# Attention, routed experts and a dense layer on one core: the second head pair's operands packed like the later pairs', and its q and k transposed ahead of the first scores

## The chip, the cores and the metric

The kernel runs on one core of a Trainium2 chip. The metric is the device time of one execution in microseconds, the median of several runs. TensorE is called PE here, VectorE DVE, ScalarE ACT, GpSimd POOL, SyncE SP.

## What is computed

Three layers follow one another: causal attention with a bias, a mixture of eight experts of which each token takes one, and a dense layer with a squared ReLU. The change touches only the attention, of which this is the core (B = 4 batches, H = 8 heads, S = 576 tokens, D = 64):

```python
scores = scale * np.matmul(q, k.transpose(0, 1, 3, 2))
cum = np.cumsum(np.maximum(s, 0.0), axis=-1)
bias = -(cum[:, :, :, None] - cum[:, :, None, :])
scores = np.where(causal, -1000000000.0, scores + np.minimum(bias, 0.0))
attn = np.exp(scores - np.max(scores, axis=-1, keepdims=True))
attn = attn / (np.sum(attn, axis=-1, keepdims=True) + 1e-09)
return np.matmul(attn, v).astype(np.float32)
```

## The kernel before

**Tiling.** Two heads of a batch make a pair; there are 16 pairs, numbered 0 to 15 in the code (pair 0 is called the first here, pair 1 the second). A pair's 576 query rows are cut into blocks of 128, and the blocks of both heads into seven units, run in the order `order=[0, 1, 3, 11, 2, 10, 4]`: units 0 and 1 hold the block of both heads, units 2, 3, 10 and 11 one block of one head, and unit 4 holds the last rows of both heads, the tail, in a PSUM tile of two banks (`ps_2`, tag `s2`, one buffer). A unit runs through scores on PE (`emit_s`), mask and maximum on DVE (`emit_m`), exponential on ACT (`emit_e`), transposes on PE (`emit_t`), their copy to SBUF (`emit_v`); then come the products with v (`emit_pv`), and the output of the pair is transposed and stored.

**Operands.** q and k are loaded by `load_qk` (six DMA issues a pair), transposed on PE in three parts (`qk_pe`: q, k, and the tails of both), and split by `qk_hi` on ACT and `qk_lo` on DVE into a rounded part and its remainder, so that fp32r matmuls give scores with enough digits. `st_a` (three buffers) and `st_b` (two) hold them. For pairs below `ND = 2` the 64 rows of a head and the rows of the other lie side by side: q of head 0 stands in the upper half of `st_a`, q of head 1 in the lower half of `st_b`, the other halves are set to zero on POOL, and a score block takes four passes: high by high, high by low, low by high, and one with `cum_q` and `cum_k` that adds the bias. From pair 2 on each head has high and low parts stacked over all 128 partitions with the rows of the bias from DRAM beside them (`aug_d`), so that two passes do. To get there, `copy_b` copies head 1's rows to `st_b` on POOL, `spread_b` and `spread_a` move 64 partitions to the other 64 by DMA (288 KB each), and `load_aug` fetches the bias rows of a head. `spread_a` overwrites rows that `spread_b` and `copy_b` read.

**Order.** The order on every engine is written out by hand: `at(key, fn)` notes a step, and `emit_tasks` emits all steps by rising key; each engine runs its own in that order, and SP issues its DMAs in that order, waiting in place for what a DMA needs. A pair has seven keys; pair p's first score has the key 7p - 2.85. The preparation (constants, running sums, the first pair's operands, loads of the second pair's q and k and of v) stands ahead of all keys; warm-up matmuls on ones fill PE's pauses there. With the keys of before, SP runs behind the preparation: q and k of pair 2 (-9.83) and pair 3 (-3.99), the gate weights `wp` (0.3, in `init_rest`), q and k of pair 4 (3.01), v of pair 2 (3.59), `load_aug` for head 1 and `spread_b` of pair 2 (6.11 and 6.16), q and k of pair 5 (7.01), `spread_a` and `load_aug` for head 0 of pair 2 (9.66). Pair 1's q and k are transposed between the first pair's units (0.87, 2.16 and 2.43), from PSUM tiles of the ring of three with the tag `t`.

Of the kernel before, what the change touches and what calls it, by code (L numbers as in the profile page):

```python
# [12 lines left out]
F32 = mybir.dt.float32  # L13
# [11 lines left out]
P = 128  # L25
# [57 lines left out]
    xt0=2.2,  # L83
    xt1=1.3,
    hv=0.9,
    q1=4.32,
)


# [1 line left out]
def attention_moe_ffn_kernel(  # L91
# [22 lines left out]
    SP = NB * P  # L114
    HP = H // 2
    NPAIR = B * HP
    ND = 2
    NO = K_['NO']
    MC = NT // P
    CAPS = [352, 320, 304, 304, 288, 288, 272, 256]  # L120
# [52 lines left out]
    def new_half(pool, key, slot):  # L173
        halves[key] = pool.tile([P, 2, 4096], F32R, tag=slot, name=slot)
# [42 lines left out]
    def at(key, fn, *args):  # L217
        tasks.append((key, len(tasks), fn, args))
# [232 lines left out]
    with tc.manual_schedule():  # L451
        with ExitStack() as actx:
# [37 lines left out]
            def bank(r):  # L490
                if r == "s":
                    return ps_s.tile([P, 512], F32, tag="s", name="s")
                if r == "o":
                    return ps_o.tile([P, 512], F32, tag=o_tag, name=o_tag)
                return ps_t.tile([P, 512], F32, tag="t", name="t")
# [46 lines left out]
            qk_ps = {}  # L542

            def qk_pe(pp, part):
                ps = qk_ps[pp, part] = bank(K_["ring"][part])
                if part < 2:
                    t = raw_q[pp][:, part * QM:(part + 1) * QM]
                    for c in range(NB - 1):
                        nc.tensor.transpose(ps[:, c * P:(c + 1) * P], t[:, c * P:(c + 1) * P], ident)  # L549
                else:  # L550
                    nc.tensor.transpose(ps[:, 0:2 * TAIL], raw_q.pop(pp)[:, 2 * QM:], ident)
# [556 lines left out]
            with tc.tile_pool(name="prep", bufs=1) as prep:  # L1108
# [50 lines left out]
                for a in range(2):  # L1159
                    nc.gpsimd.memset(rs_t[a], 1.0)  # L1160
                for a in range(2):
                    nc.gpsimd.memset(st_b[a][0:64, 1].bitcast(F32), 0.0)
                nc.gpsimd.memset(carry, 0.0)
                nc.gpsimd.memset(carryb, 0.0)
                nc.gpsimd.memset(tbl, 0.0)
                nc.gpsimd.memset(wp, 0.0)
                nc.gpsimd.memset(st_a[1][64:128, 0:3:2].bitcast(F32), 0.0)
                nc.gpsimd.memset(st_b[1][0:64, 0:3:2].bitcast(F32), 0.0)
                load_qk(1)
                load_v(0)  # L1170
                for part in range(3):
# [5 lines left out]
                        qk_lo(0, part)  # L1177
                qk_lo(0, 2)
                for r in range(2 * ND):
                    if r < ND:  # L1180
                        nc.scalar.activation(
                            out=cum_q[:, r], in_=cum_r.bitcast(F32), func=AF.Copy, scale=sel[:, r:r + 1])
                    else:
                        nc.gpsimd.tensor_scalar(
                            out=cum_q[:, r], in0=cum_r.bitcast(F32), scalar1=sel[:, r:r + 1], scalar2=None,
                            op0=ALU.mult)
                nc.scalar.copy(out=tri, in_=mt)
                nc.scalar.copy(out=iota_r, in_=ii)
                nc.scalar.copy(out=iota8, in_=ii[:, 0:E])
                nc.scalar.copy(out=iota8p, in_=ii[:, E:2 * E])  # L1190
                nc.sync.dma_start(out=aug_d[0].rearrange("c r t -> (c r) t"), in_=cum_k.bitcast(F32))
                nc.sync.dma_start(
                    out=aug_d[1, 0:2].rearrange("c r t -> (c r) t"), in_=cum_r[0:2 * NH].bitcast(F32))
# [12 lines left out]
            def init_rest():  # L1206
# [9 lines left out]
                nc.vector.tensor_single_scalar(out=ij, in_=ij, scalar=63, op=ALU.bitwise_and)  # L1216
                nc.vector.tensor_copy(out=idab[:, :, :, 1], in_=ij)
                nc.vector.memset(idab[TAIL:P, :, NB - 1], 0.0)
                for hd in range(2):
                    for i, w in enumerate((w_gate, w_ogate)):  # L1220
                        nc.sync.dma_start(
                            out=wp[64 * hd:64 * hd + 64, :, 16 * hd + 8 * i:16 * hd + 8 * i + 8],
                            in_=w.rearrange("(j h p) e -> h p j e", h=2, p=64)[hd])
# [4 lines left out]
                oT.extend(more[:, a] for a in range(NO - 2))  # L1228

            at(0.3, init_rest)  # L1230
            new_half(wpool1, (0, "a"), "w0")
            new_half(wpool1, (0, "b"), "w1")

# [2 lines left out]
            at(NU * ND + 0.5, init_spare)  # L1236

            def early(pp):
                return min(NU, 3 * max(pp - ND, 0))

            for pp in range(NPAIR):
                base = NU * pp
                t0 = base - NU
                if pp >= 2:
                    at(max(t0 + K_["ldqk"] - early(pp), t0 - 2 * NU + K_["scq"] - early(pp - 2) + 0.2), load_qk, pp)
                    at(t0 + K_["ldv"], load_v, pp)
                if pp >= 1:
                    if pp >= ND:
                        at(t0 + K_["sck"] - early(pp), scale_tail, pp, nc.gpsimd)
                    else:  # L1250
                        at(K_["od"][0], scale_tail, pp, nc.vector)
                    for part in range(3):
                        tq = t0 + K_["qk"][part] - early(pp) + (0 if pp >= ND else K_["q1"])
                        at(tq, qk_pe, pp, part)
                        at(tq + K_["qkh"], qk_hi, pp, part)
                        at(tq + K_["qkl"], qk_lo, pp, part)
                if pp >= ND:
                    tb = t0 + max(K_["dup"], K_["qk"][2] + K_["qkl"] - early(pp) + 0.4)
                    at(tb - 0.05, load_aug, pp, 1)
                    at(tb - 0.04, copy_b, pp)  # L1260
                    at(tb, spread_b, pp)
                    at(tb - K_["dup"] + K_["dupa"], spread_a, pp)
                    at(tb - K_["dup"] + K_["dupa"], load_aug, pp, 0)
                end = pp == NPAIR - 1
                units, vact, pv = (K_["l" * end + nm] for nm in ("order", "vact", "pv"))
                for i, un in enumerate(units):
# [557 lines left out]
```

## Time and profile before

| what | value |
|---|---|
| median of three runs | 862.3 us (861.71 to 862.62) |
| the profiled execution's own time | 862.74 us |
| its span | 861.0 us |
| PE busy | 843.1 us, 98% |
| DVE, ACT, POOL busy | 520.4, 452.3, 262.1 us |
| first scores of the pairs 0, 1, 2, 3 begin at | 8.94, 24.05, 39.38, 52.16 us |
| attention's scores end at about | 215 us |

Times in the rows are microseconds from the span's start. In a timeline a row is an instruction, or several of one kind merged, with its start and its duration; matmuls are pipelined, so that the difference of two starts tells more than a duration. SPq stands for SP's queue of DMA issues. The granted clock of a stretch is the share of PE's clock that the chip let through.

### The profile page before, as it was taken

The page shows a single profiled execution, that of the slowest core. Times are in us where ns is not written, and L with a number is a line of the kernel's source. Part 1 is how long each engine was busy: PE and PEld are TensorE (multiplying, and loading weights), DVE is VectorE, ACT ScalarE, POOL GpSimd, SP SyncE. Part 2 cuts the span into 40 slices and gives each one's busy share as a digit, 9 for nine tenths or more (in the row PEclk, how much of TensorE's full clock was granted, in tenths as well). Part 3 has the DMA queues.
Part 4 walks back from the last instruction along what each step waited for, and adds up shares of the span by engine and source line. Part 5 has one row for each costly group of instructions (what it writes and reads, how often), then busy time and mean ns, then how long its engine had stood idle before and what let it go on. Part 6 is the DMA issues. An engine that isn't in the chain of part 4 may idle for free.

```text
span 861.0 us, 15161 instructions
## 1 busy us (share of the span) xinstructions
PE 843.1 (98%) x5412; PEld 748.7 (87%) x5412; DVE 520.4 (60%) x1180; ACT 452.3 (53%) x1012; POOL 262.1 (30%) x304
## 2 busy tenths in 40 slices
PE   8999999999999999999999999999999999999995
PEld 6876777777799999999999999999999999999994
DVE  7667777978777677768976767664233343232221
ACT  7787878988465446566655545443233232233221
POOL 6322334543126465566422232331101011001001
PEclk9999999999999999999999999999999999999999
DMA  7676677753287898999983433321010121001001
GB/s 168 137 162 142 144 183 180 178 127 91 78 278 232 255 252 266 233 280 274 296 246 96 147 120 101 100 84 62 13 62 37 37 75 38 1 1 37 1 0 40
DMA packets 113029, 113.14 MB, mean 131 GB/s; under 512 B 66034, under 2 KB 83954, under 8 KB 112947
## 3 DMA queue, kind: packets, MB, share of 16 engines
q1 hardware_dynamic: 104962, 96.68, 42.1%
q0 software_dynamic: 3664, 9.62, 3.3%
q10 hardware_dynamic: 4320, 5.80, 2.0%
q8 instruction: 45, 0.74, 0.4%
q14 instruction: 38, 0.30, 0.1%
HBM read 80.50 MB, written 23.32 MB: 121 GB/s over the span
## 4 chain that ended last, share of the span: by engine, by line
PE 47%; issue 31%; DVE 6%; ACT 6%; POOL 5%; DMA 4%; POOLq 1%; SPq 0%; ACTq 0%; DVEq 0%
PE z L1431 14%; PE z L1482 7%; PE z L1473 6%; PE s L636 5%; PE t L733 5%; PE t L696 4%; DMA cv<-in_moe_w_out_dram 2%; ACT p L680 2%; POOL out_dram L1541 1%; DVE w L250 1%; POOL cvm L1400 1%; PE t L549 1%; POOL cvm L1399 1%; ACT sta L576 1%; DMA w_out_d<-cvm 1%
## 5 line engine op out<-in xcount | busy, mean ns | idle before, releaser
L1431 PE MATMUL z<-xt,w 128*128 128x384 f32 (+6 forms) x1920 | 329.7, 320 | 0.7 <-DVE h L1442 0.6
L1431 PEld LDWEIGHTS z<-xt,w 128*128 128x128 f32 x1920 | 308.1, 188 | 9.8 <-DVE h L1442 1.2
L1482 PE MATMUL z<-w,h 128*128 128x512 f32 x864 | 214.9, 393 | 0.0
L1482 PEld LDWEIGHTS z<-w,h 128*128 128x128 f32 x864 | 160.7, 188 | 29.3
L1451 DVE SCALAR_TENSOR_TENSOR r<-z,r 128x384 f32<-128x384 f32 x96 | 53.3, 556 | 127.2 <-ACT r L1450 127.2
L1450 ACT ACTIVATE r<-z 128x384 f32<-128x384 f32 x96 | 47.2, 492 | 150.3 <-PE z L1431 149.3
L1473 PE MATMUL z<-h,w 128*128 128x304 f32 (+5 forms) x768 | 111.3, 294 | 0.4 <-DVE h L1442 0.2
L1473 PEld LDWEIGHTS z<-h,w 128*128 128x128 f32 x768 | 104.0, 189 | 1.2 <-ACT h L1441 0.4
L1399 POOL TENSOR_TENSOR cvm<-cvm,cva 128x512 f32<-128x512 f32 x32 | 43.5, 1361 | 170.6 <-DVE cva L1395 121.9
L1541 POOL DMA_INDIRECT out_dram<-ysb,tok_m x18 | 17.4, 969 | 245.5 <-ACT ysb L1528 183.2
L1458 DVE TENSOR_TENSOR h<-r,h 128x384 fp32r<-128x384 f32 x96 | 61.0, 636 | 50.3 <-ACT h L1457 49.7
L680 ACT ACTIVATE p<-p,nm 128x128 f32<-128x128 f32 (+3 forms) x144 | 84.3, 590 | 3.7 <-DVE nm L663 2.3
L1457 ACT CAST h<-r 128x384 fp32r<-128x384 f32 x96 | 49.3, 513 | 64.1 <-DVE r L1451 63.8
L250 DVE TENSOR_TENSOR w<-stg,w 128x1024 fp32r<-128x1024 f32 x49 | 75.1, 1534 | 5.4 <-ACT w L246 5.4
L663 DVE CUSTOM_DVE_ANT_0 p<-s,mask 128x128 f32<-128x128 f32 (+3 forms) x128 | 59.7, 486 | 30.4 <-PE s L636 29.3
L696 PE MATMUL t<-ident,p 128*128 128x128 f32 x400 | 69.1, 283 | 2.8 <-DVE sta L580 1.1
L246 ACT CAST w<-stg 128x1024 fp32r<-128x1024 f32 x49 | 51.4, 1049 | 22.0 <-POOL cvm L1400 18.2
L696 PEld LDWEIGHTS t<-ident,p 128*128 128x128 f32 x400 | 44.4, 140 | 18.7 <-ACT p L680 6.2
L597 POOL CAST stb<-sta 64x1152 fp32r<-64x1152 f32 x28 | 31.4, 1150 | 79.7 <-PE s L636 46.3
L1400 POOL TENSOR_TENSOR cvm<-cvs,cvm 128x512 f32<-128x512 f32 x32 | 54.2, 1694 | 2.5
L636 PE MATMUL s<-sta 128*64 128x288 f32 (+4 forms) x204 | 50.0, 342 | 0.9 <-DVE sta L580 0.9
L715 ACT COPY pt<-t 128x512 f32<-128x512 f32 (+1 forms) x94 | 47.0, 515 | 7.3 <-PE t L733 4.1
(242 smaller groups left out, 1024.8 us busy)
## 6 DMA issues: line engine op xcount, KB each, us to landing
stg<-in_moe_w_dram SPq DMA_DIRECT2D x42, 512.0 KB
cv<-in_moe_w_out_dram SPq DMA_DIRECT2D x16, 512.0 KB
stx<-in_moe_w_dram SPq DMA_DIRECT2D x14, 512.0 KB
cv<-in_moe_w_in_dram SPq DMA_DIRECT2D x14, 512.0 KB
xr<-yT_d SPq DMA_DIRECT2D x8, 768.0 KB
qk<-in_q_dram SPq DMA_DIRECT2D x32, 128.0 KB
v<-in_v_dram SPq DMA_DIRECT2D x32, 128.0 KB
stg<-in_moe_w_dram SPq DMA_DIRECT2D x16, 256.0 KB
```

The lines of the kernel that those rows point to most:

```text
L250: nc.vector.tensor_tensor(out=lo, in0=raw.pop(job), in1=hi.bitcast(F32), op=ALU.subtract)
L636: nc.tensor.matmul(ps[0:mw, d0:d0 + nn], lhsT=ql[r, m0:m0 + mw], rhs=kl[r, c0:c0 + nn], start=(i == 0 and (tail or n == 0)), stop=(done an ...
L663: nc.vector.tensor_tensor_reduce(out=dst, in0=src, in1=msk, scale=-1.0, scalar=3.0e38, op0=ALU.add, op1=ALU.min, accum_out=nm[:, c:c + 1])
L680: nc.scalar.activation(out=pt[:, cs], in_=pt[:, cs], func=AF.Exp, scale=-1.0, bias=nm[:, c:c + 1], accum_out=rs[:, r:r + 1])
L696: nc.tensor.transpose(tp[:, i * P:(i + 1) * P], pt[:, j0:j0 + P], ident)
L1399: nc.gpsimd.tensor_tensor(out=m, in0=m, in1=a.bitcast(F32), op=ALU.mult)
L1400: nc.gpsimd.tensor_tensor(out=m, in0=sq, in1=m, op=ALU.add)
L1431: nc.tensor.matmul(ps[:, 0:n], lhsT=wa[:, zw, kk, fl * P:(fl + 1) * P], rhs=xt[:, zx, kk, 0:n], start=(i == 0), stop=(i == 3 * KD - 1))
L1451: nc.vector.scalar_tensor_tensor(out=gg, in0=ps[:, 0:TT], scalar=0.0, in1=gg, op0=ALU.max, op1=ALU.mult)
L1458: nc.vector.tensor_tensor(out=ht[:, 1], in0=gg, in1=ht[:, 0].bitcast(F32), op=ALU.subtract)
L1473: nc.tensor.matmul(y_acc[g][d][:, 0:n], lhsT=wb[:, zw, fl, d * P:(d + 1) * P], rhs=ht[:, zh, 0:n], start=(f == 0 and i == 0), stop=(f == n ...
L1482: nc.tensor.matmul(acc, lhsT=ht[:, zh, c * P:(c + 1) * P], rhs=wb[:, zw, fl, :], start=(first and i == 0), stop=(last and i == 2))
```

## The change

`ND` becomes 1: only the first pair keeps the four passes, and the second is packed as all later ones. Its zeros are no longer set, `cum_q` holds two rows instead of four, both made on ACT, and four small casts of constants move from ACT to POOL. `st_b`'s second buffer gets a wider stretch of zeros. The second pair's q and k are transposed with the keys -2.87 and -2.86, just ahead of the first score (-2.85), into the two banks of the tail's PSUM tile; their high and low parts and the tails follow up to -0.15. Its moves get keys from -0.9 to -0.08 in the order `load_aug` for head 1, `copy_b`, `spread_b`, `spread_a`, `load_aug` for head 0. The load of pair 3's q and k moves from -3.99 to 0.5, and the gate weights from 0.3 to 2.0. The spare output buffers, which reuse `cum_q`'s memory, are made at 7.5 instead of 14.5. Keys of later pairs stay.

```diff
-    q1=4.32,
+    q1=[[-2.87, -2.84, -2.15], [-2.86, -1.2, -1.1], [-1.0, -0.2, -0.15]],
...
-    ND = 2
+    ND = 1
...
             def qk_pe(pp, part):
-                ps = qk_ps[pp, part] = bank(K_["ring"][part])
+                if pp == 1 and part < 2:
+                    if part == 0:
+                        qk_ps[pp] = ps_2.tile([P, 1024], F32, tag="s2", name="s2")
+                    ps = qk_ps[pp][:, 512 * part:512 * part + 512]
+                else:
+                    ps = bank(K_["ring"][part])
+                qk_ps[pp, part] = ps
...
-                    nc.gpsimd.memset(st_b[a][0:64, 1].bitcast(F32), 0.0)
+                    nc.gpsimd.memset(st_b[a][0:64, 1:2 + a].bitcast(F32), 0.0)
...
-                nc.gpsimd.memset(st_a[1][64:128, 0:3:2].bitcast(F32), 0.0)
-                nc.gpsimd.memset(st_b[1][0:64, 0:3:2].bitcast(F32), 0.0)
...
                 for r in range(2 * ND):
-                    if r < ND:
-                        nc.scalar.activation(
-                            out=cum_q[:, r], in_=cum_r.bitcast(F32), func=AF.Copy, scale=sel[:, r:r + 1])
-                    else:
-                        nc.gpsimd.tensor_scalar(
-                            out=cum_q[:, r], in0=cum_r.bitcast(F32), scalar1=sel[:, r:r + 1], scalar2=None,
-                            op0=ALU.mult)
-                nc.scalar.copy(out=tri, in_=mt)
-                nc.scalar.copy(out=iota_r, in_=ii)
-                nc.scalar.copy(out=iota8, in_=ii[:, 0:E])
-                nc.scalar.copy(out=iota8p, in_=ii[:, E:2 * E])
+                    nc.scalar.activation(
+                        out=cum_q[:, r], in_=cum_r.bitcast(F32), func=AF.Copy, scale=sel[:, r:r + 1])
+                nc.gpsimd.tensor_copy(out=tri, in_=mt)
+                nc.gpsimd.tensor_copy(out=iota_r, in_=ii)
+                nc.gpsimd.tensor_copy(out=iota8, in_=ii[:, 0:E])
+                nc.gpsimd.tensor_copy(out=iota8p, in_=ii[:, E:2 * E])
...
+            def load_wp():
...
+            at(2.0, load_wp)
...
             def early(pp):
-                return min(NU, 3 * max(pp - ND, 0))
+                return min(NU, 3 * max(pp - 2, 0))
...
-                    at(max(t0 + K_["ldqk"] - early(pp), t0 - 2 * NU + K_["scq"] - early(pp - 2) + 0.2), load_qk, pp)
+                    tq = max(t0 + K_["ldqk"] - early(pp), t0 - 2 * NU + K_["scq"] - early(pp - 2) + 0.2)
+                    at(0.5 if pp == 3 else tq, load_qk, pp)
...
-                    if pp >= ND:
+                    if pp >= 2:
                         at(t0 + K_["sck"] - early(pp), scale_tail, pp, nc.gpsimd)
...
                     for part in range(3):
-                        tq = t0 + K_["qk"][part] - early(pp) + (0 if pp >= ND else K_["q1"])
+                        if pp == 1:
+                            for t1, fn in zip(K_["q1"][part], (qk_pe, qk_hi, qk_lo)):
+                                at(t1, fn, pp, part)
+                            continue
+                        tq = t0 + K_["qk"][part] - early(pp)
...
                 if pp >= ND:
                     tb = t0 + max(K_["dup"], K_["qk"][2] + K_["qkl"] - early(pp) + 0.4)
-                    at(tb - 0.05, load_aug, pp, 1)
+                    if pp == 1:
+                        tb = K_["q1"][2][2] + 0.05
+                    at(tb - 0.05 if pp > 1 else -0.9, load_aug, pp, 1)
                     at(tb - 0.04, copy_b, pp)
                     at(tb, spread_b, pp)
-                    at(tb - K_["dup"] + K_["dupa"], spread_a, pp)
-                    at(tb - K_["dup"] + K_["dupa"], load_aug, pp, 0)
+                    ta = tb - K_["dup"] + K_["dupa"]
+                    if pp == 1:
+                        ta = tb + 0.02
+                    at(ta, spread_a, pp)
+                    at(ta, load_aug, pp, 0)
```

## Rows read from the trace of the kernel before

**Rows 1.** The page: each engine's busy us, share, instructions.

```profile
PE 843.1 (98%) x5412; PEld 748.7 (87%) x5412; DVE 520.4 (60%) x1180; ACT 452.3 (53%) x1012; POOL 262.1 (30%) x304
```

**Rows 2.** Stretches by pair: length, engines' busy us (count), granted clock, DMA share, GB/s.

```profile
24.00:39.40 15.40, 15.40 (x124) 13.28 (x122) 9.70 (x33) 10.98 (x32) 5.60 (x7) 1.00 0.71 155
39.40:52.20 12.80, 12.02 (x99) 9.70 (x96) 8.65 (x31) 10.68 (x31) 3.26 (x5) 1.00 0.73 168
52.20:64.20 12.00, 11.79 (x94) 9.15 (x92) 8.28 (x31) 9.88 (x30) 3.37 (x5) 1.00 0.66 152
```

**Rows 3.** Timeline of SP's queue: start, duration, engine, line, transfer, count.

```profile
6.10 0.61 SPq L515 DMA_DIRECT2D qk<-in_k_dram  x1
...
15.78 0.61 SPq L515 DMA_DIRECT2D qk<-in_k_dram  x1
16.48 1.10 SPq L512 DMA_DIRECT2D qk<-in_q_dram  x2
17.63 0.61 SPq L515 DMA_DIRECT2D qk<-in_q_dram  x1
18.28 1.14 SPq L512 DMA_DIRECT2D qk<-in_k_dram  x2
...
22.85 1.98 SPq L512 DMA_DIRECT2D qk<-in_q_dram  x2
...
29.86 0.64 SPq L584 DMA_DIRECT2D stb<-sta  x1
...
34.73 0.62 SPq L584 DMA_DIRECT2D sta<-sta  x1
35.39 0.49 SPq L539 DMA_DIRECT2D sta<-aug_d  x1
```

**Rows 4.** Timeline of PE, second pair; matmuls of one kind merged.

```profile
24.05 0.56 PE L636 MATMUL s<-sta 128*128 128x192 f32 x3
...
25.01 0.60 PE L549 MATMUL t<-ident,qk 128*128 128x128 f32 x4
...
27.53 0.95 PE L636 MATMUL s<-sta 128*128 128x512 f32 x3
...
28.54 0.38 PE L696 MATMUL t<-ident,p 128*128 128x128 f32 x2
...
35.98 0.64 PE L636 MATMUL s<-sta,stb 128*128 128x288 f32 x3
...
38.27 0.87 PE L733 MATMUL t<-pt,v 128*64 128x256 f32 x8
...
39.38 0.45 PE L636 MATMUL s<-sta 128*128 128x192 f32 x2
```

**Rows 5.** Timeline of PE at the start; in brackets idle time and releaser.

```profile
7.16 1.06 PE L549 MATMUL t<-ident,qk 128*128 128x128 f32 x4
...
8.94 0.51 PE L636 MATMUL s<-sta 128*128 128x192 f32 x1
10.37 0.74 PE L636 MATMUL s<-sta 128*128 128x192 f32 x2 [0.93 <-DVE sta L580]
...
12.89 0.84 PE L636 MATMUL s<-sta,stb 128*128 128x256 f32 x3
13.53 0.41 PE L636 MATMUL s<-cum_k,cum_q 128*128 128x256 f32 x1
13.74 0.93 PE L636 MATMUL s<-sta 128*128 128x512 f32 x3
```

**Rows 6.** Timeline of ACT in the first pair: last exponential of the second unit.

```profile
14.96 0.50 ACT L680 ACTIVATE p<-p,nm 128x256 f32<-128x256 f32 x1
```

**Rows 7.** Timeline of POOL from 15 to 31 us.

```profile
20.59 0.53 POOL L521 TENSOR_SCALAR qk<-qk 64x128 f32<-64x128 f32 x1 [3.52 <-DMA qk<-in_k_dram]
27.31 2.24 POOL L597 CAST stb<-sta 64x1152 fp32r<-64x1152 f32 x2 [6.19 <-DVE sta L580]
```

**Rows 8.** Timeline of PE in the third pair's stretch.

```profile
43.28 0.30 PE L551 MATMUL t<-ident,qk 128*128 128x128 f32 x1 [0.78 <-issue]
```

## The prediction

> **What bounds the kernel now.** I read the page's first part, then the stretches by pair, then PE's timeline around the second pair, then SP's queue over the same time. PE is busy for 98% of the span [rows 1]; the reader is to see that a saving on PE is worth its full time wherever PE has no pauses. In the second pair's stretch it has none: 15.40 of 15.40 us, with ACT at 10.98 and DVE at 9.70 [rows 2]. The next two stretches have 0.78 and 0.21 us of idle PE. So the four-pass scores of the second pair lie on the path that sets the end. The second view to read for this change is SP's queue [rows 3]: from 15.78 to 35.88 us, over thirty issues of which the rows show the first, the last and some between, each begins where the one before ends; a large one takes about 0.6 us, a pair's q and k six of them. SP is as full as PE there, and what the diff adds to the second pair is four more issues on SP.
>
> **What is removed from PE.** Packed like the later ones, the second pair runs two passes a block instead of four. Its start times give the price [rows 4]: the first unit of 8 passes runs from 24.05 to 25.01, so half is 0.48 us; the second unit (256 columns) I take at the same 0.5; a unit with 512 columns runs from 27.53 to 28.54, half 0.5, and there are two; the two with 384 columns lie between, 0.39 each; the tail of 16 passes runs from 35.98 to about 38.2, half 1.1. Together 0.48 + 0.5 + 1.0 + 0.78 + 1.1 = 3.9 us for 24 matmuls; since a block's first pass starts slower than its later ones and stays, I take 3.6. The second pair would reach the end of its scores some 3.6 us earlier, if its operands and those of the third pair are there.
>
> **What is moved ahead of the first scores.** The eight q and k transposes of the second pair come on PE behind the last warm-up matmuls, at about 9.1 us. There PE is at the low clock: three matmuls with 256 columns take 0.64 us from 12.89 to 13.53, 0.213 each, which is 1.2 GHz [rows 5]. Four transposes took 1.06 with the drain of the last [rows 5], so eight take 1.7 us (at most 2.1) and end at about 10.8. PE stood idle there for 0.93 us until 10.37 waiting for DVE, behind one pass of 0.21 [rows 5]; of the 1.7 us some 1.3 fill that. The first scores shift by about 0.6 us, and the transposes no longer stand later, where eight at the high clock are some 0.9. About even. The q and k data are not late: the last issue of k is done at 6.71 on SP [rows 3], a landing of 2.3 to 3.0 us from its start (below, step 2) makes 8.4 to 9.1, and PE wants k at 9.9. The small casts go from ACT, which waits there anyway, to POOL, which loses two memsets and two scalings. DVE does three more subtractions ahead of the constants of init_rest, which delays the fourth unit's reduction by about 1 us; with the earlier hidden behind the wait below, I put nothing down for it, and 0.6 us where that cover is gone (bounds 0 and 1.7).
>
> **What is added on SP, step by step.** New order behind the third pair's q and k: rows for the second head (load_aug 1), spread_b, spread_a, rows for the first head (load_aug 0), and only then the fourth pair's q and k, the gate weights, the fifth pair's q and k, v, and the third pair's own moves with the sixth pair's q and k between them.
> 1. The third pair's q and k end at 16.39 [rows 3]. A load_aug takes 0.49, so spread_b starts at about 16.95 and ends at 17.6. It needs the second pair's last copy on ACT, which stands behind the second unit's exponentials; those start at 14.96 before [rows 6] and about 0.6 later after, so the copy is done by about 16.3 and does not hold it.
> 2. spread_a overwrites what spread_b reads, so it waits on SP until spread_b has landed, and until POOL has copied (2.24 us [rows 7], from about 16.7 to 19). How long a move takes to land is not shown by any wait. From below: a fetch of the fourth pair, issued at 17.63 or 18.28, let POOL start at 20.59, so 2.3 to 3.0 us from the start of its issue [rows 3, 7]. From above: spread_a of the third pair was issued at 34.73 and its first score began at 39.38 without a pause [rows 3, 4], so under 4.65. A move is 288 KB against 32 or 128; at the 155 to 168 GB/s of these stretches [rows 2] that is about another 1 us. I take 3.7: landed at 20.65, and SP has stood for 3.0 us (bounds 1.7 and 4.0). Behind it in the queue wait the fourth pair's fetches and all that follows.
> 3. spread_a and the last load_aug take about 1.2 us: SP is free at 21.9, where before the fourth pair's fetch began at 16.48. That is a shift of 5.4 us.
> 4. What follows up to the third pair's last load_aug took from 16.48 to 35.39 before, 18.9 us without a pause [rows 3]. All of it stays. Two issues of it were long (1.98 for two at 22.85, against 1.10 at 16.48), which may have been waits that a later start removes: I take 0.6 off (bounds 0 and 1.2). The third pair's last load_aug then starts at 35.39 + 4.8 = 40.2 instead of 35.39.
> 5. It lands 3.2 us later (below: the fetch's 2.3; above: 35.39 to 39.38, 4.0): 43.4. The third pair's first score needs all of these rows. It began at 39.38, and would begin at 43.4: 4.0 us later (bounds +1.1, all low ends together, and +6.3, all high ones).
>
> The second pair's own moves are in time or nearly so: load_aug lands at about 21.3 + 3.2 = 24.5 against its first score at 24.05 plus what the start costs.
>
> PE, with 3.6 us less to do, arrives at the third pair's first score at about 24.6 + 15.3 - 3.6 = 36.3 and stands idle for some 7 us. The saving turns into a wait, and the wait goes on for longer than the saving. Behind the blocked score stand the second pair's last transposes and the third pair's whole stretch.
>
> The Trainium skill has a fit for one DMA, in DMA: Bandwidth & Descriptors, section Anatomy of one DMA: 2.0 us plus its bytes over 436 GB/s, measured for GpSimd's path. By it 288 KB would be an estimated 2.7 us; SP would stand 1.0 us less and the last rows land 1.2 us sooner, a sum 2.2 us lower than mine. Between the row's bounds I stay with the rows.
>
> **The clock after the pause.** PE at the start, having stood idle, runs at 1.2 GHz; the pace changes in the group of 512 columns at 13.74, after unbroken work from 10.37 [rows 5]. A pause of 0.78 us in the third pair is the longest later one, and PE has its high pace behind it [rows 8]. A pause of 7 us is not in the trace. I put it with the program's start: the clock falls, and unbroken work from 10.37 to 13.74, 3.4 us, shows what it costs to come back: half of it, 1.7 us (bounds 0, and 3.3 for the low stretch from 7.16 on, half of 6.6). The Trainium skill, in TensorE: Matmul & The Clock Gate, section Why this matters for your kernels, warns of losing the clock in a long pause between bursts; no run here shows it yet.
>
> **What comes back.** The third stretch took 12.80 us against 12.00 for the fourth, with 0.78 us idle [rows 2]. After a pause in which ACT, DVE and POOL empty, most of that idle goes: -0.5 (0 to -0.8). SP's lateness does not reach the fourth pair: a pair has 6 issues for q and k, 3 for v, 4 moves and 2 stores, 15 at 0.6 make 9 us, and its stretch has 12.
>
> **Sum.** +4.0 + 1.7 - 0.5 = +5.2 us on the profiled span of 861.0: 866.2. That execution took 862.74, 1.7 more than its span; the median of the runs is 862.3, so +5.2 gives 867.5.
>
> **The rivals.**
> 1. The wait as above, but the clock holds. For it: no fall anywhere after the start; against it: the pause would be nine times the longest seen. Without the 1.7: 865.8.
> 2. The other side: SP is not what ends last. spread_a's wait for spread_b's landing is the one price on which this turns. If moves land in the low 2.3 us and the issues behind it, free of their waits, catch up, the last load_aug would land at 40.5; to be faster, the total shift on SP must stay under about 1 us, against 2.3 us for four issues alone, or the third pair must have more slack than rows 3 and 4 show. For it: the 4.0 us from issue to score may be mostly slack. Then PE's saving stays: 862.3 - 3.6 + 0.6 = 859.3. It holds if the third pair's last load_aug lands before PE arrives, between 36.3 and 39.
> 3. About even: the shift on SP is near 2.5 us, slack takes 1 to 1.5 of it, no clock is lost: 862.3 within 1.7.
> 4. That the change doesn't do what it says: eight transposes and two-pass scores are plain in the diff; only a second pair held up at 24.5 by its own moves would undo it, which case 1 hides. No chance of its own.
>
> **How the numbers follow.** My forecast with the clock lost 0.45, rival 1 0.27, rival 2 0.14, rival 3 0.12, and 0.02 for both bounds high, above 870.5. The predicted time is that of the likeliest, 867.5. The range of 8 in 10 takes in the forecast and rival 1 with their bounds and part of rival 3: 861.4 to 870.5. A measurement here can tell 0.2%, 1.7 us: faster below 860.6, 0.14; same to 864.0, 0.14 (rival 3 and the lowest end of rival 1); slower 0.72.
>
> **What would show it.** In the changed profile: the second pair's units with two passes, its stretch without cum_q; eight transposes ahead of the first score; on SP a pause of some 3 us between spread_b and the first spread_a, then issues without a break up to the third pair's last load_aug near 40; the third pair's first score near 43, with an idle PE of 6 to 7 us ended by that DMA; behind it matmuls of 256 columns at 0.21 us, or a granted clock under 1. Wrong would be: a third pair that starts before 39 with no pause (steps 2 to 5 fail), SP with gaps behind the moves (it was not full), or a long pause with no slow pace after it (rival 1).

## The result, and the profile after

The kernel after takes 867.36 us (median of four runs, 866.67 to 868.44), the one before, run beside it, 862.0 us (861.32 to 862.62): a ratio of 1.0070 [1.0058, 1.0082], 5.4 us slower. The forecast was 867.5 and 5.2 us. The profiled execution of after took 866.67 us, the least of its four; that of before took 862.74, more than the others of before. Read against each other these two give 3.9 us.

The page, span and busy times (against [rows 1]):

```profile
span 864.9 us, 15116 instructions
PE 841.2 (97%) x5388; PEld 747.0 (86%) x5388; DVE 519.5 (60%) x1177; ACT 450.4 (52%) x1005; POOL 261.2 (30%) x307
```

PE has 24 matmuls fewer, as counted in the prediction, and is busy for 1.9 us less, though the span is longer.

The stretches of after (length; PE, PEld, DVE, ACT, POOL busy; granted clock; DMA share; GB/s), against [rows 2]: the second pair, the pause, the third pair, the fourth.

```profile
24.00:36.00 12.00, 12.00 (x97) 9.52 (x96) 9.04 (x29) 9.92 (x29) 4.12 (x6) 1.00 0.58 123
36.00:43.60 7.60, 2.46 (x20) 1.71 (x19) 2.32 (x8) 2.37 (x7) 3.35 (x4) 0.79 0.85 180
43.60:56.00 12.40, 11.79 (x79) 9.95 (x80) 7.08 (x27) 8.57 (x25) 0.11 (x1) 0.86 0.65 147
56.00:68.00 12.00, 11.80 (x93) 9.15 (x92) 8.28 (x30) 9.88 (x30) 3.31 (x5) 1.00 0.68 152
```

Before the third pair PE is busy for only 2.46 of 7.60 us, and from there into the third pair the granted clock is 0.79 and 0.86, where before it was 1.00.

SP's queue in after (start, duration, line, transfer), against [rows 3], and its longest wait between 15 and 46 us (waiting line, releaser, total, times, longest):

```profile
16.46 0.44 SPq L539 DMA_DIRECT2D stb<-aug_d  x1
17.00 0.64 SPq L590 DMA_DIRECT2D stb<-sta  x1
20.24 0.62 SPq L590 DMA_DIRECT2D sta<-sta  x1
20.95 0.45 SPq L539 DMA_DIRECT2D sta<-aug_d  x1
21.49 1.45 SPq L512 DMA_DIRECT2D qk<-in_q_dram  x2
...
39.12 0.62 SPq L590 DMA_DIRECT2D sta<-sta  x1
39.80 0.48 SPq L539 DMA_DIRECT2D sta<-aug_d  x1
```

```profile
SPq L590 <- DMA stb<-sta: 2.5, 1, 2.5
```

The four issues of the second pair stand behind the third pair's q and k. Between the first move's end at 17.64 and the second's start at 20.24 SP issues nothing; then no gap is left up to the third pair's last row fetch at 39.80, which began at 35.39 before [rows 3].

PE in after, matmuls of one kind merged, in brackets idle time and releaser (against [rows 4, 5]):

```profile
9.11 1.29 PE L555 MATMUL s<-ident,qk 128*128 128x128 f32 x8
10.16 0.71 PE L642 MATMUL s<-sta 128*128 128x192 f32 x3
...
17.12 0.34 PE L642 MATMUL s<-cum_k,cum_q 128*128 128x384 f32 x1
20.11 1.12 PE L702 MATMUL t<-ident,p 128*128 128x128 f32 x4 [2.66 <-ACT p L686]
...
25.80 0.45 PE L642 MATMUL s<-sta 128*128 128x192 f32 x2
...
37.79 0.55 PE L702 MATMUL t<-ident,p 128*128 128x128 f32 x3
43.48 0.71 PE L642 MATMUL s<-sta 128*128 128x192 f32 x2 [5.14 <-DMA sta<-aug_d]
...
57.82 0.45 PE L642 MATMUL s<-sta 128*128 128x192 f32 x2
209.51 0.45 PE L642 MATMUL s<-sta 128*128 128x192 f32 x2
```

The reader is to see four things: eight transposes ahead of the first score; a pause of 2.66 us in the first pair, which the prediction did not have; the pause of 5.14 us that the third pair's last rows end; and two matmuls of 192 columns that take 0.71 us behind it, against 0.45 in the fourth pair. The last pair's first score is at 209.51, in before at 203.82, 5.7 us earlier:

```profile
203.82 0.45 PE L636 MATMUL s<-sta 128*128 128x192 f32 x2
```

In the experts' stage, between 300 and 440 us, 1.2 us of that distance is lost again: there PE pauses in before for 0.43 us at 385.06, and a pause between 0.6 and 2.0 us stands at some such place in about half of the profiles below. It does not follow the attention's edits; the experiments are therefore read by the start times in the attention as well as by the time.

### The profile page after: what moved, and what is told of

It reads as the page before. It is cut to its first block, busy times and chain, and to the rows that moved or that the text cites. A ratio compares the mean times of both kernels' runs of the same rounds, so it can differ in the third digit from the quotient of the medians.

```text
span 864.9 us, 15116 instructions
## 1 busy us (share of the span) xinstructions
PE 841.2 (97%) x5388; PEld 747.0 (86%) x5388; DVE 519.5 (60%) x1177; ACT 450.4 (52%) x1005; POOL 261.2 (30%) x307
## 4 chain that ended last, share of the span: by engine, by line
PE 55%; issue 30%; ACT 4%; DVE 3%; POOL 2%; POOLq 1%; DMA 0%; DVEq 0%; ACTq 0%
PE z L1443 19%; PE z L1485 11%; PE z L1494 7%; PE t L739 5%; PE s L642 4%; PE t L702 3%; ACT p L686 2%; POOL out_dram L1553 1%; PE z L333 1%; ACT sta L582 1%; PE t L555 1%; PE s L777 1%; ACT pt L721 1%; PE z L1077 1%; PE z L1105 1%
## 5 line engine op out<-in xcount | busy, mean ns | idle before, releaser
L603 POOL CAST stb<-sta 64x1152 fp32r<-64x1152 f32 x30 | 33.7, 1151 | 82.3 <-PE s L642 56.1
```

## The experiments

The theory: the second pair's moves delay SP, the third pair's last rows come late, PE waits and then runs at the low clock. The rivals: the order of the fetches did it, or the longer start did it (PE, or the lost clock there). The runs, with the first scores read from PE's timelines. Each ratio is against before as run beside that kernel.

| kernel | us | ratio | second pair | third pair (its pause) | last pair |
|---|---|---|---|---|---|
| before | 862.0 | | 24.05 | 39.38 | 203.82 |
| after | 867.36 | 1.0070 [1.0058, 1.0082] | 25.80 | 43.48 (5.14) | 209.51 |
| e1_moves_first | 863.40 | 1.0020 [1.0007, 1.0033] | 25.83 | 38.13 | 204.41 |
| e2_fetch_first | 866.74 | 1.0052 [1.0032, 1.0072] | 28.04 | 43.93 (3.35) | 209.78 |
| e3_no_standing | 865.34 | 1.0046 [1.0033, 1.0058] | 25.82 | 41.24 (2.89) | 205.65 |
| e4_filled_pause | 868.22 | 1.0071 [1.0047, 1.0094] | 25.57 | 44.66 (1.37) | 209.12 |
| e5_moves_first_consts_late | 862.74 | 1.0014 [0.9997, 1.0030] | 24.67 | 38.36 | 204.06 |
| e6_sp_delay_alone | 870.24 | 1.0090 [1.0065, 1.0115] | 23.06 | 44.86 (6.23) | 211.44 |
| e7_reordered | 862.84 | 1.0008 [0.9994, 1.0022] | 23.57 | 35.86 | 202.81 |
| e8_reordered_filled | 864.83 | 1.0030 [1.0014, 1.0047] | 23.55 | 36.58 | 203.74 |
| e9_reordered_weights | 859.96 | 0.9979 [0.9967, 0.9990] | 23.68 | 35.96 | 200.99 |
| e10_split_fetch | 860.12 | 0.9971 [0.9954, 0.9987] | 21.83 | 35.55 (0.43) | 201.03 |

### The cause alone, in the kernel before

e6_sp_delay_alone is the kernel before with nothing but eight small fetches more on SP, whose data nobody reads.

```diff
+            def extra(n):
+                for i in range(n):
+                    t = apool_x.tile([64, 2, D], F32, tag="xx", name="xx")
+                    nc.sync.dma_start(out=t, in_=q[0, 0:2, S - TAIL:S, :].rearrange("h p d -> p h d"))
+
+            at(0.2, extra, 8)
```

> The kernel before, with eight more DMA issues on SP (the tails of a head pair's q into tiles that nothing reads) ahead of the gate weights, 0.65 us each, 5.2 us in all; PE's work is that of before. Theory (SP is full up to the third pair's last load_aug, and that sets its start): spread_a and load_aug of the third pair are issued near 40.0 and 40.6 us instead of 34.73 and 35.39, its first score begins near 44.2 instead of 39.38 with a pause of some 4.8 us, the clock may fall behind it, and the time is 4.5 to 6.5 us above before. Rival (the third pair's rows have slack, and the loss in the changed kernel lies in what the second pair's new steps do on DVE and POOL): under 2 us above before.

SP's queue and PE's wait in this kernel, and its stretches of the pause and the third pair (columns as above):

```profile
20.11 5.60 SPq L1236 DMA_DIRECT2D xx<-in_q_dram  x8
...
41.19 0.49 SPq L540 DMA_DIRECT2D sta<-aug_d  x1
```

```profile
44.86 0.71 PE L637 MATMUL s<-sta 128*128 128x192 f32 x2 [6.23 <-DMA sta<-aug_d]
```

```profile
38.00:44.80 6.80, 0.63 (x7) 0.31 (x3) 0.71 (x3) 1.14 (x3) 1.69 (x4) 0.68 0.73 163
44.80:59.70 14.90, 14.65 (x94) 12.20 (x95) 8.08 (x30) 9.96 (x28) 1.80 (x2) 0.80 0.64 147
```

Issues of 5.60 us move the last row fetch by 5.8 (41.19 against 35.39 [rows 3]) and the third pair's first score by 5.48 (44.86 against 39.38 [rows 4]), nearly one for one. The missing 0.32 us is slack that before had: from that issue to the score it took 3.99 us, here 3.67. In after it is 3.68 us and in e3 below 3.57, so the bytes that were added did not slow the landing. The third pair's stretch then takes 14.91 us, 2.1 more than the 12.78 of before, at a granted clock of 0.80. That makes 7.6 us at the last pair and 8.1 in the time, above the 4.5 to 6.5 expected: the theory put the third pair 0.7 us too early and gave too little for the clock. A delay on SP, with no other part of the change, makes a loss of this kind and more.

### The third pair's moves ahead of the fetches behind them

e1_moves_first takes the gate weights, the fifth and sixth pairs' q and k and v out of SP's way.

```diff
-            at(2.0, load_wp)
+            at(25.0, load_wp)
...
-                    at(0.5 if pp == 3 else tq, load_qk, pp)
-                    at(t0 + K_["ldv"], load_v, pp)
+                    at({3: 0.5, 5: 11.12, 6: 14.75}.get(pp, tq), load_qk, pp)
+                    at({2: 9.75, 3: 14.7}.get(pp, t0 + K_["ldv"]), load_v, pp)
```

> The changed kernel with SP's queue put in another order: the third pair's moves ahead of its v, of the sixth pair's q and k and of the gate weights. Theory (SP's lateness sets the third pair's start): the third pair's last load_aug is issued near 34.5 us instead of 39.8, its first score begins near 38.2 instead of 43.5, PE's pause of 5.1 us is under 0.5, no low clock behind it, and the time falls by 5.3 us for the wait and some 1.8 for the clock, from 867.4 to about 860.3, below the 862.0 of before. Rival (the loss is made in the first pair, by PE's pause of 2.7 us at 17.4 to 20.1 and the low clock behind it): that pause stays, and the time stays above 864.

SP and PE in this kernel:

```profile
34.28 0.45 SPq L539 DMA_DIRECT2D sta<-aug_d  x1
```

```profile
20.31 1.11 PE L702 MATMUL t<-ident,p 128*128 128x128 f32 x4 [2.64 <-ACT p L686]
38.13 0.45 PE L642 MATMUL s<-sta 128*128 128x192 f32 x2
64.76 0.44 PE L642 MATMUL s<-sta 128*128 128x192 f32 x2 [1.57 <-DMA sta<-aug_d]
```

The last row fetch starts at 34.28 instead of 39.80, the third pair at 38.13 without a pause: 5.4 us of the third pair's delay are gone, by an edit of SP's order alone, and the time falls from 1.0070 to 1.0020. It does not go below before as expected. What the late rows had covered now shows: the first pair's pause of 2.64 us, which ends on ACT's exponentials and is followed by the low clock (0.62 from 19.5 to 24 us). And the fetches that were put off make a new wait of 1.57 us in the fifth pair.

### The order of the fetches

e2_fetch_first puts the fourth pair's q and k back where before had them, ahead of the second pair's moves.

```diff
-                    at(0.5 if pp == 3 else tq, load_qk, pp)
+                    at(tq, load_qk, pp)
```

> The changed kernel with the fourth pair's q and k fetched ahead of the second pair's moves, as before. Theory (the sum of issues and the standing wait on SP count, not this order): spread_b is issued near 20.7, spread_a near 24, the second pair's own rows land near 28, so that PE waits there some 2 to 3 us; the third pair's last load_aug stays near 39.8 and its first score near 43.5; the time within 1.5 us of 867.4. Rival (the fetch of the fourth pair that was moved behind the moves is what makes the queue late): the third pair's first score comes some 3.5 us sooner, the time near 863.

PE in this kernel:

```profile
28.04 0.44 PE L642 MATMUL s<-sta 128*128 128x192 f32 x2 [2.27 <-DMA sta<-aug_d]
43.93 0.71 PE L642 MATMUL s<-sta 128*128 128x192 f32 x2 [3.35 <-DMA sta<-aug_d]
```

The third pair starts at 43.93, as late as in after (43.48); only now the second pair waits too. The moved fetch is not the cause: the four added issues and the standing are there in either order.

### The standing alone

e3_no_standing issues `spread_a` behind the fourth pair's q and k, so that SP works while the first move lands.

```diff
-                        ta = tb + 0.02
+                        ta = 0.6
```

> The changed kernel with the fourth pair's q and k between spread_b and spread_a of the second pair, so that SP has work while spread_b lands. Theory: SP's pause of 2.6 us between spread_b and spread_a is gone; the second pair's rows are issued near 22 and land near 24.5, before it needs them at 25.8; the third pair's last load_aug is issued near 37.2 and its first score begins near 40.9, 2.6 us sooner, with a pause of some 2.5 us instead of 5.1; the time falls by 2.6 to 4.4 us, the more if the clock holds: 863 to 864.8. Rival (the issues alone make SP late, not the standing wait): under 1 us.

PE, and the third pair's stretch:

```profile
41.24 0.44 PE L642 MATMUL s<-sta 128*128 128x192 f32 x2 [2.89 <-DMA sta<-aug_d]
```

```profile
41.20:54.00 12.80, 11.97 (x95) 9.67 (x96) 8.14 (x30) 9.68 (x28) 1.91 (x2) 1.00 0.72 169
```

The last row fetch starts at 37.67 instead of 39.80 (2.1 us, against a standing of 2.6), the third pair at 41.24 instead of 43.48 (the second pair now waits 1.08 us for its own rows, but the third pair's rows still end last), and this time the clock holds behind a pause of 2.89 us: the stretch takes 12.78 us, as in before. At the last pair 3.9 us come back, in the time 2.0 (865.34 against 867.36). The start times bear the theory out; the time came out a little above what was expected, and the difference lies behind the attention, where this profile has a pause of 0.66 us at 413.96.

### The pause filled

e4_filled_pause puts 24 matmuls on ones into the pause, to hold the clock.

```diff
+            at(11.14, warm, 24, 512, "t")
```

> The changed kernel with 24 matmuls of ones with 512 columns (5.1 us at 2.4 GHz) on PE just ahead of the third pair's first score, in the pause; their result is not used. Theory (the pause costs its length and then the clock): the third pair still starts near 43.5 us, since its rows land then; the clock doesn't fall behind it, and the stretch from the third to the fourth pair's first score takes some 12.6 us instead of 14.34; the time falls by about 1.7 us, from 867.4 to 865.7. Rival (the clock's fall cost nothing, the longer stretch has another cause): the stretch stays over 14 and the time within 0.5 us of 867.4.

PE, a pair of SP's issues, and the third pair's stretch:

```profile
37.95 5.34 PE L500 MATMUL t<-onesb 128*128 128x512 bf16 x24
44.66 0.44 PE L642 MATMUL s<-sta 128*128 128x192 f32 x2 [1.37 <-DMA sta<-aug_d]
```

```profile
37.71 1.85 SPq L512 DMA_DIRECT2D qk<-in_k_dram  x2
```

```profile
44.60:57.40 12.80, 11.95 (x94) 9.66 (x95) 8.14 (x30) 9.68 (x28) 1.90 (x2) 1.00 0.74 171
```

Behind the filled pause the clock is 1.00 and the stretch takes 12.77 us (44.66 to 57.43), against 14.34 in after (43.48 to 57.82). So the lost clock costs 1.57 us. The time did not fall, because SP's last row fetch was 1.2 us later here: two pairs of issues were long, such as the 1.85 us above against 1.14 for the same pair in after. Why they were long, this run does not show; the worth of the clock is shown for the stretch and not for the time.

### The first pair's pause

e5_moves_first_consts_late is e1 with the constants of `init_rest` behind the first pair's reductions on DVE.

```diff
-            at(0.3, init_rest)
+            at(2.9, init_rest)
```

> As the kernel with the moves first, and the constants of init_rest 2.6 keys later, off the time in which POOL copies the second pair's operands. Theory: PE's pause of 2.7 us in the first pair comes from the constants (3.3 us on DVE beside POOL's copies, 1.7 us in the kernel before); without them ahead of the fourth unit it is under 1 us and the clock doesn't fall there; the second pair then starts when its own moves have landed, near 24.2 instead of 25.8, so 1.6 us are gained: about 858.7. Rival (the pause is due to the subtractions of the second pair that now stand on DVE ahead): the pause stays over 2 us and the time within 0.5 us of the kernel with the moves first.

PE in this kernel:

```profile
24.67 0.71 PE L642 MATMUL s<-sta 128*128 128x192 f32 x2 [3.48 <-DMA sta<-aug_d]
```

The pause of 2.6 us in the first pair is gone; PE reaches the second pair at 21.19, 24.67 less 3.48, where e1 starts it at 25.83 (the first scores began 0.75 us earlier in e5; e7 below compares without that). But then the second pair's own rows are late, its fetch issued at 21.10, and a pause of 3.48 us with the low clock behind it takes most of the gain. The theory of the first pair's pause held; the 858.7 us expected from it did not come, and against before the time is about even. The second pair has the same fault as the third: its rows stand behind an SP that is full and stands.

### A better order

e7_reordered is e5 with the second pair's first row fetch in the preparation, the third pair's q and k between the two moves, and the fetches of later pairs spread out.

```diff
-                    at({3: 0.5, 5: 11.12, 6: 14.75}.get(pp, tq), load_qk, pp)
-                    at({2: 9.75, 3: 14.7}.get(pp, t0 + K_["ldv"]), load_v, pp)
+                    at({2: -0.09, 3: 0.5, 4: 7.0, 5: 11.12, 6: 14.75, 7: 21.65}.get(pp, tq), load_qk, pp)
+                    at({2: 9.75, 3: 14.7, 4: 18.12}.get(pp, t0 + K_["ldv"]), load_v, pp)
...
-            at(25.0, load_wp)
+            at(25.2, load_wp)
...
-                    at(tb - 0.05 if pp > 1 else -0.9, load_aug, pp, 1)
+                    at(tb - 0.05 if pp > 1 else -9.9, load_aug, pp, 1)
```

> The changed kernel with SP's order made anew for the first five pairs: the second pair's moves ahead of the third pair's q and k where their data is there, each fetch in the time in which a spread lands, gate weights and far fetches later, and the constants late. Theory: spread_b of the second pair is issued near 14.5 us, its last load_aug near 19.5, its first score begins near 23.3 instead of 25.8 (24.05 before), the third pair's near 35.4 (39.38 before), the fourth's near 47.6 (52.16 before), and 4 us remain: about 857.5, below the 861.5 to 862 of before. Rival (a packed second pair is held up whatever SP's order, since its moves must land between the first pair's scores and its own): the second pair starts after 25, and the time is not below before.

PE in this kernel, and then its waits between 60 and 80 us:

```profile
23.57 0.44 PE L642 MATMUL s<-sta 128*128 128x192 f32 x2 [1.84 <-DMA sta<-aug_d]
```

```profile
PE t L834 <- DMA wp<-n_moe_w_output_gate_dram: 2.4, 1, 2.4
```

The third pair starts at 35.86, 3.5 us ahead of before. At 71.8 us PE then waits for something new: the gate weights now come too late. Of the 4 us that were expected to remain, 1.0 is left at the last pair and nothing in the time (1.0008). e8_reordered_filled adds eight matmuls on ones ahead of the second pair, for the clock:

```diff
+            at(4.14, warm, 8, 512, "t")
```

> As the reordered kernel, with eight matmuls of ones (1.7 us) on PE ahead of the second pair's first score. Theory: where the reordered kernel has a pause of about 2 us there and loses the clock for some 3 us behind it, this one keeps the clock and is up to 1.7 us faster; where that one keeps its clock anyway, the two are within 0.5 us. Rival (the matmuls of ones come late or wait for a bank): the second pair starts later by up to 1.7 us and the time is higher by as much.

PE in this kernel, at the second matmul of the second pair:

```profile
24.37 0.36 PE L642 MATMUL s<-sta 128*128 128x192 f32 x1 [0.49 <-DMA sta<-sta]
```

The second pair starts at 23.55 as without them, the third 0.7 us later (36.58). The clock had not been lost behind e7's pause of 1.84 us, where two matmuls take 0.44 us, so the filler had nothing to keep. The 0.7 us is a new wait behind the second pair's first matmul, for the rows that `spread_a` moves; it was issued at the same time as in e7 (19.33 against 19.32), and why it landed later here the run does not show. e9_reordered_weights is e7 with the gate weights earlier.

```diff
-            at(25.2, load_wp)
+            at(18.13, load_wp)
```

> The reordered kernel with the gate weights fetched some 15 us sooner, ahead of the fifth pair's spread_a. Theory: PE's wait of 2.4 us for the gate weights at 71.8 us is gone, nothing else in the first pairs moves by over 0.5 us, the last pair's first score begins near 200.4 instead of 202.81 (203.82 before), and the time falls by some 2.4 us against the reordered kernel: about 2 us below before. Rival (the wait hides another at the same place, or the weights now hold up the fifth pair): the last pair's first score stays after 202, and the time is not below before by more than the interval.

PE in this kernel:

```profile
23.68 0.44 PE L642 MATMUL s<-sta 128*128 128x192 f32 x2 [1.87 <-DMA sta<-aug_d]
...
35.96 0.45 PE L642 MATMUL s<-sta 128*128 128x192 f32 x2
```

The wait for the weights is gone, and the time is 0.9979 [0.9967, 0.9990] of before: the packing of the change, with SP's order rebuilt around it and the constants moved, is faster than both kernels. Of the 3.4 us that the third pair is ahead of before, 2.8 are left at the last pair and 1.5 in the time; where all of the rest goes is not shown. e10_split_fetch then fetches only q of the third pair between the two moves, and k behind them.

```diff
+                    if pp == 2:
+                        at(-0.09, load_qk, 2, (0,))
+                        at(0.4, load_qk, 2, (1,))
+                    else:
...
```

> As that kernel, with only q of the third pair, and not q and k, issued on SP between the second pair's spread_b and spread_a. Theory: spread_a is issued when spread_b has landed, near 17.7 us instead of 19.3, the second pair's first score begins near 22 instead of 23.6 and PE's pause there is under 0.5 us; another 1.5 us remain if the third pair's k is still in time: about 3.5 us below before. Rival (the third pair's k, later by some 1.2 us, or its moves now end last): the third pair's first score stays near 35.9 and the time is that of the kernel without the split.

PE in this kernel:

```profile
21.83 0.44 PE L646 MATMUL s<-sta 128*128 128x192 f32 x2 [0.50 <-DMA sta<-aug_d]
23.06 0.63 PE L559 MATMUL t<-ident,qk 128*128 128x128 f32 x4 [0.57 <-DMA qk<-in_k_dram]
...
35.55 0.44 PE L646 MATMUL s<-sta 128*128 128x192 f32 x2 [0.43 <-DMA sta<-aug_d]
```

The second pair starts 1.85 us earlier than in e9: the wait is 1.37 us shorter, and PE, whose first scores began sooner here, arrives 0.48 us sooner. By the third pair 0.4 is left, since its k and its rows come later, and the last pair is where it was. Its ratio, 0.9971 [0.9954, 0.9987], is not to be told from e9's; the 3.5 us expected below before did not come.

## Why the prediction was right, step by step

The mechanism was the forecast's: SP ends last, the third pair's rows are late, PE waits, the clock falls.

1. `spread_b`'s start: 16.95 forecast, 17.00 measured. ACT did not hold it.
2. SP's standing: 3.0 us forecast, 2.6 measured. `spread_a` was issued 3.24 us after `spread_b`, where 3.7 was taken; e1, e2 and e5 show 3.23, 3.4 and 3.4. By the Trainium skill, in DMA: Bandwidth & Descriptors, section Anatomy of one DMA, whose fit was measured for GpSimd's path, the landing would have been an estimated 2.7 us. The measurement lies about midway between that and the value taken.
3. The shift on SP: 5.4 us forecast, 5.0 measured (21.49 against 16.48 [rows 3]).
4. The way to the last row fetch: 18.9 less 0.6 forecast, 18.3 measured (21.49 to 39.80). It starts at 39.80, where 40.2 was said.
5. From that issue to the first score: 3.2 us forecast, 3.7 measured. So 43.48 stands against 43.4: two errors, 0.4 us too much in step 2 and 0.5 too little in step 5, cancel. The term of +4.0 measured +4.1.

The clock: 1.7 us forecast, 1.57 measured (14.34 less e4's 12.77), in the middle of its bounds. The rule of the Trainium skill that was weighed, in TensorE: Matmul & The Clock Gate, section Why this matters for your kernels, agrees with the pause of after: 5.14 us of idle PE, granted clock 0.79 and 0.86 around its end. PE works at a granted clock of 0.50 from 43.48 to about 47.2 us, 3.7 us, and the prediction had taken half of 3.4 from before's start. That start is a poor source: the low pace up to 13.74 [rows 5] stands in no other profile here, and in e6 the clock cost 2.1 us, so the size was met in part by luck.

What comes back: -0.5 forecast, nothing measured. This is the term that failed. The idle time that was to vanish, the 0.78 us on "issue" in the third pair [rows 8], is there with and without a pause ahead of it, 0.61 us in after, 0.79 in e4 and 0.78 in e3, and the stretches of e3 and e4 take 12.78 and 12.77 us as in before. Where the clock held, empty engines ahead of a stretch did not take it away. Behind a low clock part of it goes, 0.17 us in after and more in e6, where 0.19 is left; that is already inside the 1.57 and 2.1.

Together the three terms measured 4.1 + 1.6 + 0, the 5.7 us by which the last pair is late, where 5.2 were forecast. The time is longer by 5.4 us, and in the two profiles a part of the 5.7 is lost again behind the attention, which the prediction did not reckon with; that forecast and time differ by only 0.2 us is in part luck.

PE's arrival: 36.3 forecast, 38.34 measured (the last transposes end there), so that the pause was 5.1 us and not 7. Two steps were too low, and neither moved the end, since SP ended last. The saving of 24 matmuls was put at 3.6 us; the second pair's stretch took 12.3 to 12.5 us in after, e1 and e9, against 15.33 before, a saving of about 3.0. And the second pair began at 25.80, not 24.6. The transposes at the start took 1.05 us there (9.11 to 10.16) and were no burden; but where they had stood, they had filled a wait of PE. It arrives at the fourth unit's transposes at 17.46 (the end of the 384 columns above), and they start at 20.11, in before at 19.86 behind the second pair's q and k. The prediction put "about even" on this move and at most 1.7 us on DVE's delay; e7 shows the price without cover: with its first scores at 10.13, where e1 has 10.20, PE is at the second pair at 21.73 (23.57 less its pause of 1.84), where e1 has 25.83. That is 4.1 us: the pause of 2.64, about 1.0 for the low clock behind it (e3, where the clock held behind the same pause, has PE at the second pair at 24.74), and 0.4 not accounted for. So the step that the first pair's cost is nothing was right only under the cover of SP. Had the third pair's rows been in time, rival 2 would not have come out at 859.3: e1, which comes nearest to that case, gives 1.0020 of before, its wait in the fifth pair included.

Before's own profile hides a part of this price. It is the only one of the twelve in which PE keeps the low pace up to 13.74 us; the granted clock reads 1.00 there all the same. e6 has before's code at this place:

```profile
11.90 0.51 PE L637 MATMUL s<-sta,stb 128*128 128x256 f32 x3
...
23.06 0.56 PE L637 MATMUL s<-sta 128*128 128x192 f32 x3
```

These three matmuls take 0.84 us in [rows 5] and 0.51 here, and the second pair starts at 23.06 instead of 24.05. So after reaches its second pair 2.7 us late against e6, not 1.75. For the third pair it matters little: with the landing of 3.67 us from e6, before's last rows were there at an estimated 39.1 (35.39 + 3.67), so an earlier PE could have gained 0.3 us. SP all but set the third pair's start in before already, which is why nearly the whole shift arrived there.

Rival 1, the wait with the clock held, would be 865.8; the clock did fall. Rival 2 turned on the landing of the moves: even with the standing gone altogether (e3) the third pair is 1.9 us later than before. Rival 3, a shift near 2.5 us, is about what e3 makes (its last row fetch 2.3 us after that of before), and it is not even: 1.0046.

## What to carry to other kernels

When a queue issues without a gap for twenty microseconds, price a new step on it by the issues and by the time the queue stands for its wait, and follow that sum to the last transfer that a busy engine needs; in e6 it arrived there nearly one for one. Work that is moved out of a place may have been what filled a wait: ask what the engine does there instead, even if another delay covers it at the moment. A packing that saves engine time and adds transfers has to come with an order of the queue built for it: the same packing was 5.4 us slower in one order and faster than before, 0.9979, in another (with the constants moved too).

## What was not expected of the hardware

Small DVE operations took several times as long beside POOL's copies. Two steps of the constants in after, the same two in before with a scaling that POOL ran beside them, and POOL's copies in after:

```profile
15.25 1.04 DVE L1212 TENSOR_SCALAR ik<-ij 128x20 int32<-128x20 int32 x1
...
16.33 1.06 DVE L1213 TENSOR_SCALAR idab<-ik 128x20 bf16<-128x20 int32 x1
```

```profile
16.28 0.32 DVE L1213 TENSOR_SCALAR ik<-ij 128x20 int32<-128x20 int32 x1
...
16.63 0.23 DVE L1214 TENSOR_SCALAR idab<-ik 128x20 bf16<-128x20 int32 x1
```

```profile
16.54 0.54 POOL L521 TENSOR_SCALAR qk<-qk 64x128 f32<-64x128 f32 x1
```

```profile
15.11 2.24 POOL L603 CAST stb<-sta 64x1152 fp32r<-64x1152 f32 x2 [3.22 <-DVE sta L586]
```

Two POOL copies of 1.12 us each end at about 16.23 and 17.35; the two DVE steps end at 16.29 and 17.39. In e7, where POOL is not copying at that time, the same two take 0.17 and 0.18 us. The Trainium skill, in SBUF — State Buffer, section SBUF: two separate sides, says that DVE and POOL share a pair of ports, and that a POOL operation, or a DVE operation in a mode with two ports, takes it for a whole instruction and blocks the other; the ends agree with that. Not every POOL operation does it: the scaling in before runs from 16.54 to 17.08, and the second DVE step beside it still takes 0.23 us. The two steps, 2.10 us instead of 0.55, are why the fourth unit's reduction came 0.87 us later (18.52 against 17.65), not DVE's extra subtractions, which the prediction had blamed: the constants began at 14.89, in before at 15.55.

The length of a pause alone did not tell whether the clock fell. PE fell to 1.2 GHz behind pauses of 5.14 and 6.23 us, of 3.48 in e5 and 3.35 in e2, and of 2.66 and 2.64 in the first pair of after and e1. At this place in the first pair, e2 and e3 have the same pause, and only in e2 was the clock low behind it:

```profile
19.83 1.12 PE L702 MATMUL t<-ident,p 128*128 128x128 f32 x4 [2.65 <-ACT p L686]
```

```profile
20.26 0.66 PE L702 MATMUL t<-ident,p 128*128 128x128 f32 x4 [2.65 <-ACT p L686]
```

In e3 it did not fall behind the later pause of 2.89 us either. In e4, again behind 2.65, it held at first and was low about 1 us later. The low stretch lasted longer in e6 than in after (2.1 against 1.57 us lost), with the same work behind it. What decides between them stays open.
